# Two of a batch's four loads issued from ScalarE's DMA queue, in a grouped-query attention forward and backward

## The chip, the cores and the metric

The kernel runs on one core of a Trainium2 chip. A core has TensorE (matrix products; PE in the profile, PEld for its weight loads), VectorE (DVE), ScalarE (ACT), GpSimd (POOL) and SyncE (SP), each with its own instruction stream, and sixteen DMA engines that move data between HBM and SBUF. A DMA transfer is issued by an instruction on one of these streams and ends when its semaphore has received sixteen arrivals, one from each DMA engine. The metric is the device time of one execution in microseconds, lower is better; it is given as the median of several runs.

## The reference

Attention of 4 query positions against 2048 keys, 32 batches, 32 query heads on 4 key heads, and its gradients. Everything is bfloat16 at the interface.

```python
B, Hq, Hkv, Sq, Sk, D = 32, 32, 4, 4, 2048, 128
k = jnp.repeat(k, 8, axis=1); v = jnp.repeat(v, 8, axis=1)
scores = jnp.einsum("bhqd,bhkd->bhqk", q, k) * D ** -0.5
p = softmax(scores, axis=-1)
out = jnp.einsum("bhqk,bhkd->bhqd", p, v)
# returned: out, and the gradients of q, k and v for a given grad_out
```

The 8 query heads of a key head times 4 positions make 32 rows; the 4 key heads together fill 128 partitions. Each batch reads K and V (2 MB each) and writes their gradients (2 MB each), so HBM traffic is 273 MB in all, half read and half written.

## The kernel before

**Data.** The host packs K and V of a batch into two rows each: heads 0 and 1, and heads 2 and 3. A row is 128 partitions by 4096 bf16 values. The K rows are 128 values longer: the first K row carries q of the batch, the second grad_out. The gradients leave in the same form, the second dK row with dq and the second dV row with the output appended. So a batch has eight transfers of about 1 MB: four loads and four stores. In SBUF there are 20 row slots; a slot holds a loaded row, and later a row of results or another load.

**Steps of a batch.** The plan names them with two letters or a little more, a part number and a place:

- `LK` 0 and 1, `LV` 1 and 0: the loads, first and second K row, and the V rows, row 1 ahead of row 0. They are called LK0, LK1, LV1 and LV0 in what follows. `SV` 1 and 0, `SK` 0 and 1: the stores of dV and dK, called SV1, SV0, SK0 and SK1.
- `QT`, `KT`, `VT`, `ET`, `DT`: transposes on TensorE into PSUM (line 241, for q and grad_out line 230); `KTe` and so on copy the result to SBUF on ScalarE (line 207) or VectorE (line 209).
- `S`: scores (line 255); `MX`, `EX`, `RC`: maximum, exponential with row sums (ScalarE, line 264), reciprocal.
- `O`, `DQ` (line 288): output and dq. `DP`, `DL`, `DS`: gradient of the scores. `DV`, `DK` (line 310): gradients, copied out of PSUM into a result row by `DVe` and `DKe` (line 316) on ScalarE or VectorE. `dop`, `qp`, `rs` are small products on GpSimd.

**Order.** There is no loop over batches in the usual sense. `PLAN` is a string of four characters per step: name, part, place (PSUM bank, engine A or D, or SBUF slot) and tile. `plan()` turns it into a list of units, and `emit(u)` issues them one after another under a manual schedule, so the string fixes the order on every engine. Steps of three batches interleave: stores and late steps of one batch stand between early steps of the next and loads of one to three batches ahead. In the later part of the plan the eight transfers of a cycle stand in this order: SV1, LV0, SV0, LK1, SK0, LV1, LK0, SK1.

**Queue.** All transfers are issued by SyncE (`nc.sync.dma_start`, line 226 for loads, line 320 for stores), so they form one queue. The waits are put in by the framework: a load waits until the readers of its slot are done, or the store from its slot has landed, and a store waits for the copies into its row. Transfers take eight completion semaphores in turn, and a transfer also waits until the transfer that had its semaphore before, eight places earlier, has landed; with eight transfers per batch that is the same transfer of the batch before. An instruction that waits holds back everything behind it on its engine. SyncE has nothing else to do than these issues; ScalarE's stream consists of the copies of lines 207 and 316 and the exponential.

The first batch's loads are split in two halves each.

Of the kernel before, what the change touches and what calls it, by code (L numbers as in the profile page):

```python
# [160 lines left out]
def kernel(  # L161
# [11 lines left out]
    nc = tc.nc  # L173
# [40 lines left out]
    def emit(u):  # L214
        b, name, i = u.b, u.name, u.part
        t = T[b]
        if name in ("LK", "LV"):
            x = slots[int(u.where, 36)]
# [4 lines left out]
            n = LONG if name == "LK" else ROW  # L223
            src = (k_r if name == "LK" else v_r)[i][b]
            for w in (slice(0, Sk), slice(Sk, n)) if b == 0 else (slice(0, n),):
                nc.sync.dma_start(out=x[:, w], in_=src[:, w])  # L226
        elif name == "QT":
            ps = t["qtp"] = bank(u)[:, 0:P]
            for j, x in enumerate(("q", "go")):
# [4 lines left out]
        elif name in ("KT", "VT", "ET", "DT"):  # L234
# [3 lines left out]
            src = t[x, h] if h is not None else t["e" if x == "E" else "ds"][:]  # L238
            src = src.bitcast(FP32).rearrange("p (j d) -> p j d", d=P)
# [4 lines left out]
        elif name in ("S", "DP"):  # L244
# [6 lines left out]
            out = t["S"][:, 2 * QW * i:2 * QW * i + 2 * QW] if name == "S" else t["DP", i]  # L251
            x, side = ("KT", 0) if name == "S" else ("VT", 1)
# [26 lines left out]
        elif name in ("O", "DQ"):  # L279
            if i == 0:  # L280
                t[name] = bank(u)[:, 0:D]
            xt, x = ("ET", "V") if name == "O" else ("DT", "K")
# [7 lines left out]
        elif name in ("Oe", "DQe"):  # L290
            x, by, to = ("o", "rinv", "DV") if name == "Oe" else ("dq", "rs", "DK")
# [9 lines left out]
        elif name == "DS":  # L301
            w = slice(2 * QW * i, 2 * QW * i + 2 * QW)
            nc.vector.scalar_tensor_tensor(out=t["ds"][:, w], in0=t["DP", i], scalar=t["dl"][:], in1=t["e"][:, w],  # L303
                                           op0=ALU.subtract, op1=ALU.mult)
        elif name in ("DV", "DK"):
            i, g = divmod(i, 2)
# [6 lines left out]
        elif name in ("DVe", "DKe"):  # L313
            i, g = divmod(i, 2)
            copy = nc.scalar.copy if u.where == "A" else nc.vector.tensor_copy
            copy(out=heads_of(t[name[:2], "out", g])[:, :, QW * i:QW * i + QW],  # L316
                 in_=t[name[:2], i, g].rearrange("p (h c) -> p h c", h=2))
# [4 lines left out]
    with tc.manual_schedule():  # L322
        for u in units:
            emit(u)
# [37 lines left out]
```

## Time and profile before

| | us |
|---|---|
| timed runs (median, lowest, highest of 3) | 671.31, 671.30, 671.62 |
| span of the profiled execution | 671.1 |
| PE busy in it | 607.9 |
| VectorE busy | 572.0 |
| ScalarE busy | 569.6 |
| GpSimd busy | 39.0 |

The span runs from the first to the last instruction of one profiled execution; a time for this execution apart from its span is not given. The page cuts the span into 40 slices and shows the busy share of each in tenths, the granted TensorE clock, the share of the DMA engines and what they moved:

```profile
PE   6998999999998999988998989988999989898993
DMA  9999999999999999999999999999999999999867
GB/s 354 417 424 423 419 381 423 423 423 423 423 426 424 424 423 424 424 425 426 414 420 425 413 417 421 414 422 424 396 388 408 417 424 424 404 421 423 347 258 322
```

The single transfers, from issue to landing (lines of KB each and median us):

```profile
out_dram<-row SPq DMA_DIRECT2D x64, 1056.0 KB, 20.1
out_dram<-row SPq DMA_DIRECT2D x64, 1024.0 KB, 20.4
row<-in_k_dram SPq DMA_DIRECT2D x62, 1056.0 KB, 18.1
row<-in_v_dram SPq DMA_DIRECT2D x62, 1024.0 KB, 20.5
```

A transfer of 1 MB takes some 20 us from issue to landing because up to seven others stand ahead of it in the queue.

### The profile page before, as it was taken

The page shows a single profiled execution, that of the slowest core. Times are in us where ns is not written, and L with a number is a line of the kernel's source. Part 1 is how long each engine was busy: PE and PEld are TensorE (multiplying, and loading weights), DVE is VectorE, ACT ScalarE, POOL GpSimd, SP SyncE. Part 2 cuts the span into 40 slices and gives each one's busy share as a digit, 9 for nine tenths or more (in the row PEclk, how much of TensorE's full clock was granted, in tenths as well). Part 3 has the DMA queues.
Part 4 walks back from the last instruction along what each step waited for, and adds up shares of the span by engine and source line. Part 5 has one row for each costly group of instructions (what it writes and reads, how often), then busy time and mean ns, then how long its engine had stood idle before and what let it go on. Part 6 is the DMA issues. An engine that isn't in the chain of part 4 may idle for free.

```text
span 671.1 us, 20678 instructions
## 1 busy us (share of the span) xinstructions
PE 607.9 (91%) x8768; PEld 401.4 (60%) x8768; DVE 572.0 (85%) x736; ACT 569.6 (85%) x802; POOL 39.0 (6%) x102
## 2 busy tenths in 40 slices
PE   6998999999998999988998989988999989898993
PEld 5665566666665666655655655655655666565651
DVE  1988799999997999988888989887888979896994
ACT  4997899999997999888888989887888979886894
POOL 0000000000000000000000000000000000000000
PEclk9999999999998999999999999998999989998997
DMA  9999999999999999999999999999999999999867
GB/s 354 417 424 423 419 381 423 423 423 423 423 426 424 424 423 424 424 425 426 414 420 425 413 417 421 414 422 424 396 388 408 417 424 424 404 421 423 347 258 322
DMA packets 37533, 273.97 MB, mean 408 GB/s; under 512 B 4160, under 2 KB 4160, under 8 KB 5184
## 3 DMA queue, kind: packets, MB, share of 16 engines
q1 hardware_dynamic: 37440, 272.65, 98.2%
q8 instruction: 69, 1.13, 0.6%
q14 instruction: 24, 0.20, 0.1%
HBM read 136.31 MB, written 136.31 MB: 406 GB/s over the span
## 4 chain that ended last, share of the span: by engine, by line
DMA 50%; PE 37%; DVE 4%; ACT 4%; issue 3%; SPq 0%; POOL 0%; DVEq 0%; ACTq 0%; POOLq 0%
DMA row<-in_k_dram 50%; PE psum L241 19%; PE psum L310 8%; PE psum L288 5%; PE psum L255 5%; ACT row L316 3%; DVE vt_sb L209 2%; DVE ds_sb L303 1%; DVE row L316 0%; DVE e_sb L260 0%; ACT e_sb L264 0%; PE psum L230 0%; SPq L226 0%; ACT dt_sb L207 0%; DVE row L296 0%
## 5 line engine op out<-in xcount | busy, mean ns | idle before, releaser
L241 PE MATMUL psum<-ident,row 128*128 128x128 f32 x2048 | 290.1, 284 | 28.4 <-DMA row<-in_k_dram 21.5
L316 ACT CAST row<-psum 128x1024 bf16<-128x1024 f32 x292 | 289.2, 1023 | 30.9 <-PE psum L310 29.1
L241 PEld LDWEIGHTS psum<-ident,row 128*128 128x128 f32 x2048 | 224.7, 143 | 94.8 <-issue 32.0
L316 DVE CAST row<-psum 128x1024 bf16<-128x1024 f32 x220 | 264.9, 1217 | 5.7 <-PE psum L310 2.9
L207 ACT COPY kt_sb<-psum 128x512 f32<-128x512 f32 x190 | 110.2, 598 | 20.6 <-PE psum L241 20.4
L207 ACT COPY vt_sb<-psum 128x512 f32<-128x512 f32 x160 | 92.0, 602 | 35.3 <-PE psum L241 34.6
L303 DVE SCALAR_TENSOR_TENSOR ds_sb<-psum,delta,e_sb 128x1024 bf16<-128x1024 f32 x64 | 82.1, 1283 | 13.4 <-PE psum L255 9.0
L310 PE MATMUL psum<-ds_sb,qp_sb 32*128 32x512 bf16 x512 | 76.9, 383 | 3.4 <-ACT row L316 1.0
L260 DVE TENSOR_SCALAR_CACHE_REDUCE e_sb<-psum 128x2048 bf16<-128x2048 f32 x32 | 73.3, 2292 | 5.7 <-PE psum L255 5.7
L310 PE MATMUL psum<-e_sb,dop_sb 32*128 32x512 bf16 x512 | 68.8, 388 | 2.5 <-issue 1.0
L209 DVE COPY kt_sb<-psum 128x1024 bf16<-128x1024 bf16 x66 | 45.0, 685 | 28.4 <-PE psum L241 27.8
L209 DVE COPY vt_sb<-psum 128x1024 bf16<-128x1024 bf16 x96 | 60.7, 684 | 10.0 <-PE psum L241 9.8
L264 ACT ACTIVATE e_sb<-psum,m 128x2048 bf16<-128x2048 f32 x32 | 64.0, 2001 | 0.2 <-DVE e_sb L260 0.2
L271 POOL TENSOR_SCALAR dop_sb<-row,rinv 128x128 bf16<-128x128 bf16 x32 | 19.3, 603 | 605.3 <-DVE rinv L268 530.3
L241 PE MATMUL psum<-ident,ds_sb 128*128 128x128 f32 x256 | 41.8, 286 | 9.6 <-DVE vt_sb L209 7.0
L288 PE MATMUL psum<-row,dt_sb 128*32 128x128 bf16 x2048 | 43.5, 222 | 6.2 <-issue 5.6
L310 PEld LDWEIGHTS <-qp_sb 32*128 32x128 bf16 x512 | 19.4, 91 | 46.1 <-issue 42.6
L255 PE MATMUL psum<-vt_sb,qdt_sb 128*32 128x512 bf16 x512 | 40.7, 388 | 4.6 <-issue 4.5
L288 PEld LDWEIGHTS <-dt_sb 128*32 128x32 bf16 x2048 | 30.8, 95 | 22.0 <-issue 21.1
L241 PEld LDWEIGHTS psum<-ident,ds_sb 128*128 128x128 f32 x256 | 26.9, 140 | 27.2 <-DVE vt_sb L209 16.4
L207 ACT COPY dt_sb<-psum 128x512 f32<-128x512 f32 x63 | 38.4, 611 | 1.0 <-PE psum L241 0.9
L288 PEld LDWEIGHTS <-et_sb 128*32 128x32 bf16 x2048 | 30.4, 95 | 13.8 <-ACT et_sb L207 11.3
(29 smaller groups left out, 310.1 us busy)
## 6 DMA issues: line engine op xcount, KB each, us to landing
out_dram<-row SPq DMA_DIRECT2D x64, 1056.0 KB, 20.1
out_dram<-row SPq DMA_DIRECT2D x64, 1024.0 KB, 20.4
row<-in_k_dram SPq DMA_DIRECT2D x62, 1056.0 KB, 18.1
row<-in_v_dram SPq DMA_DIRECT2D x62, 1024.0 KB, 20.5
row<-in_v_dram SPq DMA_DIRECT2D x4, 512.0 KB, 9.4
row<-in_k_dram SPq DMA_DIRECT2D x2, 544.0 KB, 5.3
row<-in_k_dram SPq DMA_DIRECT2D x2, 512.0 KB, 4.4
```

What stands on the lines that cost most here:

```text
L207: nc.scalar.copy(out=out.bitcast(FP32), in_=in_)
L209: nc.vector.tensor_copy(out=out, in_=in_.bitcast(BF16))
L241: nc.tensor.transpose(out=ps[:, P * j:P * j + P], in_=src[:, 4 * half + j, :], identity=ident32[:])
L255: nc.tensor.matmul(out[r, QW * w:QW * w + QW], lhsT=t["qdt"][:, P * side + 32 * h:P * side + 32 * h + 32], rhs=t[x, NH * i + h][:, QW * w: ...
L260: nc.vector.tensor_scalar(out=t["e"][:], in0=t["S"], scalar1=-scale, scalar2=None, op0=ALU.mult, op1=ALU.min, accum_out=t["m"][:])
L264: nc.scalar.activation(out=t["e"][:], in_=t["S"], func=ACT.Exp, bias=t["m"][:], scale=scale, accum_out=t["l"][:])
L271: nc.gpsimd.tensor_scalar(out=t["dop"][:], in0=t["go"], scalar1=t["rinv"][:], scalar2=None, op0=ALU.mult)
L288: nc.tensor.matmul(t[name][r, :], lhsT=left[:, j, r, odd], rhs=right[:, 4 * i + j, :, odd], start=(i == 0 and c == 0), stop=(i == 1 and c ...
L303: nc.vector.scalar_tensor_tensor(out=t["ds"][:, w], in0=t["DP", i], scalar=t["dl"][:], in1=t["e"][:, w], op0=ALU.subtract, op1=ALU.mult)
L310: nc.tensor.matmul(acc[:, QW * (h % 2):QW * (h % 2) + QW], lhsT=t[still][rows[h], :], rhs=t[moving][rows[h], QW * i:QW * i + QW], start=Tr ...
L316: copy(out=heads_of(t[name[:2], "out", g])[:, :, QW * i:QW * i + QW], in_=t[name[:2], i, g].rearrange("p (h c) -> p h c", h=2))
```

## The change

From batch 4 on, two of the four loads of a batch, LK1 and LV0, are issued by ScalarE with `nc.scalar.dma_start`, which puts them on ScalarE's hardware DMA queue. The plan string, the slots and every computation stay. The other six transfers of a batch, and all loads of batches 0 to 3, remain with SyncE. 56 transfers move. They now stand in ScalarE's stream at the place that the plan gives them, between its copies: LK1 ahead of a copy of a V tile, LV0 ahead of a copy of a K tile.

```diff
             src = (k_r if name == "LK" else v_r)[i][b]
             for w in (slice(0, Sk), slice(Sk, n)) if b == 0 else (slice(0, n),):
-                nc.sync.dma_start(out=x[:, w], in_=src[:, w])
+                queue = nc.scalar if b >= 4 and (name, i) in (("LK", 1), ("LV", 0)) else nc.sync
+                queue.dma_start(out=x[:, w], in_=src[:, w])
```

In the compiled program of the changed kernel each of the 56 issues on ScalarE waits for the same load of the batch before (its semaphore), and in part for an older load into its slot or for GpSimd's reading of it. SyncE keeps 204 of its 260 issues; per batch their order is SV1, SV0, SK0, LV1, LK0, SK1. Otherwise the order of instructions on the engines is that of before.

## The prediction

> **What bounds the kernel now.** I read the page's DMA part first, then busy time by stage, then SP's own waits, TensorE's waits, the chain of waits, and last the issue times of single transfers.
>
> ```profile
> DMA packets 37533, 273.97 MB, mean 408 GB/s; under 512 B 4160, under 2 KB 4160, under 8 KB 5184
> q1 hardware_dynamic: 37440, 272.65, 98.2%
> q8 instruction: 69, 1.13, 0.6%
> ```
>
> One queue carries everything and its packets fill 98.2% of the sixteen engines' span. The stages (columns after the window: its length, then PE, PEld, DVE, ACT and POOL busy, clock, DMA share, GB/s):
>
> ```profile
> 100.00:255.00 155.00, 149.17 (x2188) 98.04 (x2185) 142.36 (x184) 140.02 (x199) 9.58 (x24) 0.99 1.01 424
> 255.00:606.00 351.00, 320.67 (x4669) 211.98 (x4666) 307.11 (x395) 302.36 (x430) 20.38 (x52) 0.99 1.01 417
> 606.00:671.00 65.00, 50.51 (x802) 31.72 (x802) 47.52 (x60) 48.15 (x65) 3.56 (x9) 0.92 0.81 336
> ```
>
> From 100 to 255 us compute is nearly full (PE 149 of 155) and lives on data loaded ahead: the exponential that starts a batch recurs every 18.9 us (234.44, then 253.32). From 255 to 606 us the DMA sets the pace; a batch takes 20.5 us, 17.1 batches in the stage. SP's and then TensorE's waits between 260 and 600 us (total, times, longest):
>
> ```profile
> SPq L320 <- DMA out_dram<-row: 98.3, 49, 2.2
> SPq L226 <- DMA out_dram<-row: 83.7, 17, 5.6
> SPq L226 <- DMA row<-in_v_dram: 67.4, 33, 2.1
> SPq L226 <- DMA row<-in_k_dram: 35.4, 16, 2.8
> SPq L320 <- ACT row L316: 2.7, 6, 1.0
> ```
> ```profile
> PE psum L241 <- DMA row<-in_k_dram: 14.2, 12, 2.1
> ```
>
> SP waits 285 of 340 us for transfers eight places earlier, hardly ever for data: the window of eight is always full. TensorE waits about 1.2 us a batch for one K load. The chain says which:
>
> ```profile
> 565.38 20.47 DMA row<-in_k_dram
> ...
> 585.92 20.43 DMA row<-in_k_dram
> 606.35 0.14 issue
> 606.49 1.94 PE psum L241 x16
> ```
>
> Second K load of batch 29, then of batch 30, each issued when its predecessor lands; TensorE takes up the last 0.14 us after its landing. Matched by the plan, from 255 to 606 us the second K load (LK1) lands mostly 0.2 us before its first use and the last V load (LV0) mostly 0.1 to 1.5 us, while the other V load (LV1) has 4.5 to 7 us and the first K load (LK0) 6 to 10. The change moves the two with no slack.
>
> What sets the 20.5 us is **one DMA engine**. The trace holds sixteen arrivals per transfer, one an engine. In this stage the first comes some 7.5 us after issue, the fifteenth by 13, the last at 20.5. Intervals between successive last arrivals are, by role, 2.45 to 2.54 us (medians) for loads and 2.59 to 2.70 for stores; the engine that is first needed 2.42 to 2.56 for loads and 2.44 to 2.54 for stores between 110 and 255 us, while it was never held up. So the last engine is slow on stores only, by 0.14 us each (means of the differences), and it works without a gap from 110 us until the last store lands (640.1, 642.7, 645.9, 648.5 ... 667.5, 670.0). A rearrangement can't shorten the kernel unless this engine does its 260 transfers in less time.
>
> **The change part by part.** *SP loses 56 issues* of 0.34 us (rows below), 19 us; SP's time is waiting, so 0. Its order becomes SV1, SV0, SK0, LV1, LK0, SK1, and each waits for the same transfer of the batch before; LK0 still waits for the SK1 in its slot, and SK0 now names the moved load that filled its slot batches ago, which has long landed. Six are in flight where eight were, 15 us of work for the last engine (6 x 2.57): it does not run dry, 0.
>
> *ScalarE gains 56 issues.* No ScalarE issue is in the trace. Bounds: 0, if its sequencer issues while a copy still runs, and 1.67 us, SP's longest. I take SP's median:
>
> ```profile
> 544.82 0.34 SPq L226 DMA_DIRECT2D row<-in_k_dram  x1
> ...
> 549.78 0.34 SPq L226 DMA_DIRECT2D row<-in_v_dram  x1
> ...
> 560.28 0.34 SPq L226 DMA_DIRECT2D row<-in_v_dram  x1
> ```
> ```profile
> 536.42 1.11 ACT L207 COPY vt_sb<-psum 128x512 f32<-128x512 f32 x2
> ```
>
> 0.68 us a batch. In the DMA stage ScalarE idles 351 - 302.4 = 48.6 us, 2.8 a batch, and the pace leaves 20.5 - 18.9 = 1.6: hidden. Without that cover it would be 17.1 x 0.68 = 11.6 us. From 100 to 255 us a batch grows to 19.6 us, still under 20.5, and eats lead that the DMA stage takes anyway: 0. After 606 us one issue (LV0 of batch 31) is left: **+0.3**.
>
> *The moved loads go out earlier.* ScalarE came to the place of LK1 of batch 28 at 536.42 (the copy above is the one behind it), SP issued it at 544.82; to that of LV0 at 554.60, SP at 560.28. Slots are no hindrance: from batch 8 on they last held loads, read long before; for batches 4 to 7 the store in LV0's slot landed 6 to 11 us before ScalarE came by. On a queue of their own, served in turn with SP's, the loads share with at most one transfer each and land some 2 x 2.57 + 2 = 7 us after issue, not 20. TensorE's 1.2 us waits end.
>
> *Who is late next.* The engines do the same work, so two transfers brought forward push the rest back by 2 x 2.57 = 5.1 us. LV1, with 4.5 to 7 us, takes LK1's place. For batch 29, the last inside the stage, it has 5.3 us (landing 590.9, first use 596.2): slack 0.2. Bounds: -1.6 (a batch's spare time comes back at the end) to +0.5; I take **0**, as the stores that end the kernel go through the last engine, which has no gap to give.
>
> *The last engine.* While a moved load is served in turn with a store, store packets alternate with load packets. If its slow stores come from the writing side, that time is covered. 56 loads, each beside one SP transfer, four of six of these stores: 37 x 0.14 = 5.2 us. Bounds: -9.6 us (all of its lag in the stage, 17.1 x 4 x 0.14) and +18, if each change of queue costs 0.04 us (the longest instruction fetch against their mean, below), eight packets for each of 56 loads. The mean itself leaves nothing for a change, so the value lies on the gain's side, between 0 and 5.2; I take half: **-2.6**.
>
> Sum: 671.1 + 0.3 - 2.6 = 668.8 us of span. The profiled execution's time is known by its span alone; the median of the timed runs is 671.31, 0.2 above, so **669.0 us**.
>
> How the engines serve two queues decides all this. The trace has two already: the 69 instruction fetches of q8, 64 us in all (0.6% of 16 x 671), 0.93 each (0.88 to 0.97) for 16 KB, where 8 KB takes 0.31 on q1: 0.62 of its own and one q1 packet between, though q1 had 13 to 20 us of backlog. So two queues are taken in turn, at least for a single packet; for two long queues no row shows it. With a third queue a fetch takes 0.31 us more; the chain stops on a fetch three times (62.83, 201.42, 612.43 us, some 2 us each), and only the last, when no moved load is in flight, lies after the DMA stage: 0. The Trainium skill, "DMA: Bandwidth & Descriptors", section "Queues, rings and completion order", says so too: an engine goes round the queues that have work, a packet at a time; by that rule the second rival below falls away and the forecast's sum stays, and the fetches agree with 0.93 us.
>
> **Rivals.** *1. Hidden anyway (no change).* The last engine's work is the same whichever queue feeds it, LV1 replaces LK1, and the end is where it was: 671.3. For it: no gap in that engine's arrivals; against it: only that its stores, not its loads, are slow. The Trainium skill's page just named, section "Issuing engines are not separate DMA queues", has it thus: both queues run on the same sixteen engines and only issue time is saved; by it the time would be 671.3, and nothing here contradicts it.
>
> *2. ScalarE stands at a load (slower).* Both moved loads wait for the same load of the batch before. If the engines keep to SP's queue first, so that it lands no sooner than now, ScalarE stands as SP does: 544.82 - 536.42 = 8.4 us at LK1, with the copies of V tiles behind it whose PSUM banks TensorE needs. The delay is taken once, not per batch, as the pace stays 20.5: 671.3 + 8.4 = 679.7; where the tail absorbs half, 675.5. It decides once a moved load takes over 20.5 us, the time between two issues of its kind, to land; for it, that SP's transfers take 20.4 now; against it, the fetch row.
>
> *3. ScalarE's issue is dear (slower).* Above 1.6 / 2 = 0.8 us each, compute becomes the bound of the stage: at 1.0 us 17.1 x 0.4 = 7 us, 678; SP's first issues behind one another show 0.8 to 1.7 us a few times, 0.34 nearly always.
>
> *4. The last engine loses its lag wholly:* 671.3 - 9.6 = 661.7.
>
> **Chances.** Forecast 0.37, rival 1 0.29, rival 2 0.16, rival 3 with dearer queue changes 0.13, rival 4 0.05. About 0.2% (1.3 us) is what can be told from no change. The forecast's own range is 666 to 670.5, a little of it (0.02) within 0.2%; rivals 2 and 3 are slower but for 0.02. So faster 0.40, same 0.33, slower 0.27. The range 663.5 to 678 leaves out rival 4 and the upper part of rivals 2 and 3.
>
> **What would show it.** Right: two hardware queues, the new one with 56 transfers' bytes (some 58 MB); moved loads land in about 7 us; TensorE's wait for K is gone and one for V (LV1) appears; ScalarE's DMA issues about 0.34 us with no wait before them; last arrivals of stores nearer 2.5 us. Wrong: ScalarE idle for several us ahead of its issues (rival 2), issues near 1 us (3), a batch still 20.5 us with stores at 2.6 to 2.7 (1). The prediction fails above all if DMA packets grow longer than 309 and 319 ns when two queues are interleaved.

## The result and the profile after

The change made the kernel slower: 675.52 us (median of 4, 674.87 to 676.84) against 671.46 before (median of 4, 671.30 to 672.24), ratio 1.0053, 95% interval 1.0035 to 1.0071. The profiled execution took 674.87 us, its span is 673.1. Where a run's time and span are both known, the time is mostly 1.7 to 2.5 us above the span, so the profiled execution of the kernel before, of which only the span (671.1) is known, took some 673 us, above the four runs given here (671.30 to 672.24). The two profiles are thus 2.0 us of span apart, while the medians are 4.1 apart: half of the loss can be seen in them.

The DMA part of the page of the changed kernel (queue: packets, MB, share of 16 engines):

```profile
DMA packets 37532, 273.96 MB, mean 407 GB/s; under 512 B 4160, under 2 KB 4160, under 8 KB 5184
q1 hardware_dynamic: 29376, 213.01, 76.5%
q10 hardware_dynamic: 8064, 59.64, 21.6%
q8 instruction: 68, 1.11, 0.6%
```

The same bytes now travel on two queues, and 76.5 + 21.6 = 98.1% of the engines' span is filled, as before (98.2). From the issue list, with the median from issue to landing last, and from ScalarE's order of work:

```profile
row<-in_k_dram ACTq DMA_DIRECT2D x28, 1056.0 KB, 11.1
row<-in_v_dram ACTq DMA_DIRECT2D x28, 1024.0 KB, 9.7
```
```profile
557.65 1.01 ACT L317 CAST row<-psum 128x1024 bf16<-128x1024 f32 x1
557.73 0.34 ACTq L227 DMA_DIRECT2D row<-in_v_dram  x1
558.56 1.08 ACT L207 COPY kt_sb<-psum 128x512 f32<-128x512 f32 x2
```

The moved loads land in 10 to 11 us where they took 18 to 20; ScalarE's issue takes 0.34 us, lies inside the copy that still runs, and nothing waits ahead of it. The stages, in the columns of before (length, busy times, clock, DMA share, GB/s):

```profile
100.00:255.00 155.00, 147.18 (x2186) 97.37 (x2184) 141.69 (x183) 138.85 (x199) 9.57 (x24) 1.00 1.01 424
255.00:606.00 351.00, 317.14 (x4634) 210.57 (x4632) 302.54 (x388) 294.39 (x421) 20.34 (x51) 0.97 1.01 415
606.00:673.10 67.10, 54.11 (x846) 34.38 (x842) 53.04 (x68) 53.40 (x73) 3.59 (x9) 0.96 0.81 332
```

The DMA stage moves 415 GB/s in place of 417, and at its end more compute is left: VectorE has 53.04 us of work after 606 us where it had 47.52, ScalarE 53.40 where it had 48.15. The granted clock, 0.97 in the stage where it was 0.99, doesn't explain the loss: after 606 us it is higher than before (0.96 against 0.92), and the kernel with LK1 alone moved (e1 below) had 1.00 in the stage and lost as much. Cut at 500 us, before first, then after:

```profile
255.00:500.00 245.00, 223.02 (x3276) 147.08 (x3274) 213.65 (x273) 209.90 (x299) 14.36 (x36) 0.99 1.01 417
500.00:606.00 106.00, 97.66 (x1395) 64.91 (x1393) 93.46 (x123) 92.46 (x132) 6.01 (x16) 0.98 1.01 416
```
```profile
255.00:500.00 245.00, 220.92 (x3258) 147.03 (x3260) 211.65 (x273) 206.17 (x296) 14.36 (x36) 0.97 1.01 417
500.00:606.00 106.00, 96.22 (x1384) 63.54 (x1376) 90.89 (x116) 88.22 (x126) 5.99 (x15) 0.95 1.01 411
```

Up to 500 us the DMA is as fast as before. What it loses, it loses in the last 106 us of the stage: 5 of 416 GB/s, 1.3 us. SP's waits between 260 and 600 us, and two waits between 255 and 606 us that the list of the kernel before does not show (total, times, longest):

```profile
SPq L321 <- DMA out_dram<-row: 168.5, 46, 5.2
SPq L227 <- DMA out_dram<-row: 78.9, 16, 5.6
SPq L227 <- DMA row<-in_v_dram: 34.5, 17, 2.0
SPq L321 <- DVE vt_sb L209: 14.0, 3, 4.7
```
```profile
ACT row L317 <- DMA out_dram<-row: 31.4, 17, 3.0
PE psum L311 <- ACT row L317: 27.4, 17, 2.8
```

SP still waits for transfers, not for its own time. TensorE's wait for the K load (14.2 us before) is no longer among its waits in this stage; in its place ScalarE waits once a batch, 1.8 us each, for a store to land before it may write the next result into that slot, and TensorE waits for ScalarE. By the plan this is the slot of the store SK0, which the first result copy of SV1 two batches later takes over. In the kernel before, this copy already had no time to spare: from 255 to 606 us it starts 0.08 us behind that store's landing in 13 of 17 batches. TensorE's product for it was ready less than 0.1 us earlier, so that the list puts the short wait down to TensorE:

```profile
ACT row L316 <- PE psum L310: 17.2, 34, 1.1
```

In the changed kernel it is 0.08 us in all 17, and TensorE's product was ready up to 1.7 us earlier. The store lands some 4 us later (batch 16: 386.1 us against 381.6; batch 25: 572.5 against 567.9). The exponential of batch 28 starts at 585.9 us against 581.5, that of batch 31 at 649.6 against 646.1, and the last store lands at 671.9 against 670.0.

### The profile page after: what moved, and what is told of

Its sections match the earlier page's. It is cut to its first block, busy times and chain, and to the rows that moved or that the text cites. A ratio compares the mean times of both kernels' runs of the same rounds, so it can differ in the third digit from the quotient of the medians.

```text
span 673.1 us, 20644 instructions
## 1 busy us (share of the span) xinstructions
PE 605.6 (90%) x8768; PEld 402.2 (60%) x8768; DVE 572.1 (85%) x736; ACT 565.7 (84%) x802; POOL 39.0 (6%) x102
## 3 DMA queue, kind: packets, MB, share of 16 engines
q1 hardware_dynamic: 29376, 213.01, 76.5%
q10 hardware_dynamic: 8064, 59.64, 21.6%
## 4 chain that ended last, share of the span: by engine, by line
DMA 71%; PE 20%; ACT 4%; DVE 3%; issue 1%; POOL 0%; SPq 0%; DVEq 0%; ACTq 0%; POOLq 0%
DMA row<-in_v_dram 69%; PE psum L242 10%; PE psum L311 5%; PE psum L289 3%; DMA row<-in_k_dram 3%; ACT row L317 3%; PE psum L256 2%; DVE vt_sb L209 1%; DVE ds_sb L304 1%; DVE row L317 0%; ACT kt_sb L207 0%; ACT e_sb L265 0%; ACT vt_sb L207 0%; ACT dt_sb L207 0%; DVE row L297 0%
## 5 line engine op out<-in xcount | busy, mean ns | idle before, releaser
L311 PE MATMUL psum<-e_sb,dop_sb 32*128 32x512 bf16 x512 | 63.6, 392 | 30.1 <-ACT row L317 29.7
L209 DVE COPY kt_sb<-psum 128x1024 bf16<-128x1024 bf16 x66 | 44.9, 683 | 12.1 <-PE psum L242 11.8
L311 PEld LDWEIGHTS <-dop_sb 32*128 32x128 bf16 x512 | 16.6, 91 | 53.9 <-issue 44.4
L289 PE MATMUL psum<-row,dt_sb 128*32 128x128 bf16 x2048 | 45.7, 232 | 3.2 <-issue 2.6
L256 PE MATMUL psum<-vt_sb,qdt_sb 128*32 128x512 bf16 x512 | 42.7, 406 | 3.9 <-issue 3.8
L289 PEld LDWEIGHTS <-dt_sb 128*32 128x32 bf16 x2048 | 32.9, 100 | 19.3 <-issue 18.4
## 6 DMA issues: line engine op xcount, KB each, us to landing
row<-in_k_dram ACTq DMA_DIRECT2D x28, 1056.0 KB, 11.1
```

Of the source, the lines that this page charges most:

```text
L209: nc.vector.tensor_copy(out=out, in_=in_.bitcast(BF16))
L256: nc.tensor.matmul(out[r, QW * w:QW * w + QW], lhsT=t["qdt"][:, P * side + 32 * h:P * side + 32 * h + 32], rhs=t[x, NH * i + h][:, QW * w: ...
L289: nc.tensor.matmul(t[name][r, :], lhsT=left[:, j, r, odd], rhs=right[:, 4 * i + j, :, odd], start=(i == 0 and c == 0), stop=(i == 1 and c ...
L311: nc.tensor.matmul(acc[:, QW * (h % 2):QW * (h % 2) + QW], lhsT=t[still][rows[h], :], rhs=t[moving][rows[h], QW * i:QW * i + QW], start=Tr ...
```

## The experiments

Eighteen kernels were run, each beside runs of the kernel before on the same chip (medians 671.99 us for e1 to e4, 672.21 for e5 to e8, 671.64 for e9 to e12, 672.30 for e13 to e16, 672.21 for e17 and e18). Ratios are to these, with 95% intervals. "Lengthening" below is worked out from the trace's packet records: what a packet of 8448 or 8192 B takes above 319 or 309 ns, summed and divided by sixteen engines.

The expectations name their theories. *Slot* and *critical-transfer* theory: what costs is a transfer without slack that the moved loads pass, the store SK0 first of all. *Two-queue* theory: a second queue in itself slows the engines. *Mix* and *bunching* theory: packets grow when most engines load at once, so what counts is how loads and stores mix. *End* theory: only what is left of the lag when the loads run out costs time.

**e1: only the second K load on ScalarE's queue.**

```diff
-                queue = nc.scalar if b >= 4 and (name, i) in (("LK", 1), ("LV", 0)) else nc.sync
+                queue = nc.scalar if b >= 4 and (name, i) in (("LK", 1),) else nc.sync
```

> From batch 4 on only the second K load (LK1) goes out on ScalarE's queue. Slot theory: a load brought forward pushes every transfer it passes back by one service of the slowest engine, 2.57 us; the store SK0, whose slot ScalarE's next result copy writes with 0.1 us to spare, is passed by one load instead of two, so ScalarE waits for a store's landing and the time is about half way, 672.7 to 674.5. Rival, the DMA engines lose time whenever two queues are served: also about half, 673.5. Rival, ScalarE's issue is dear: half too. By itself it tells only whether LK1 or LV0 carries the loss.

676.34 us, 1.0066 (1.0052 to 1.0080).

**e2: only the last V load.**

```diff
-                queue = nc.scalar if b >= 4 and (name, i) in (("LK", 1), ("LV", 0)) else nc.sync
+                queue = nc.scalar if b >= 4 and (name, i) in (("LV", 0),) else nc.sync
```

> From batch 4 on only the last V load (LV0) goes out on ScalarE's queue. Slot theory: SK0 is passed by one load, 672.7 to 674.5, with ScalarE waiting for a store's landing. Rivals: half the loss too. If one of the two kernels has the whole loss and the other none, the loss isn't the number of transfers that pass the store but something of that load.

672.68 us, 1.0014 (1.0002 to 1.0026). The halves are not equal: one load alone costs all that both cost, the other a third of it or less. e1 waits in stage 255 to 606 us:

```profile
ACT row L317 <- DMA out_dram<-row: 25.2, 17, 2.2
...
PEld psum L242 <- DMA row<-in_v_dram: 14.1, 14, 2.3
```

Beside the store, the load that was left on SP's queue is now late. In e2, where no wait of ScalarE for a store is listed, TensorE still waits for the K load, 17.2 us in 13 times. The number of loads that pass SK0 is not the measure of its delay: in batch 25 it lands 5.0 us later than before in e1, with one load moved, 0.6 in e2, also with one, and 4.5 in the change, with two.

**e3, e4: another slot for the late store's successor**, with the change (e3) and without it (e4). Two slots change places, so that from batch 9 on the result row of SV1 takes over the slot of the SV1 two batches before, whose store lands some 10 us earlier than SK0 (batch 16 in the change: 376.5 us against 386.1):

```diff
+        x, y = slot(used), slot(freed)
+        for key, k in at.items():
+            if starts[key] >= p:
+                units[k].where = {x: y, y: x}.get(units[k].where, units[k].where)
...
-    units = plan()
+    units = reslot(plan())
```

> The changed kernel, with two slots exchanged from about batch 6 on: the result row of SV1 takes the slot that SV1 of two batches before left (free some 10 us earlier), and the load LV1 takes the one that SK0 left. Same transfers, same queues, same instruction order. Slot theory: ScalarE's wait for stores (33 us, 20 times) nearly goes, the next limits are the slot of SV0 (1.6 to 4.2 us) and LV1 (4.5 us), and the time falls by 2 to 4 us against the changed kernel, to 671.5 to 673.5. Rivals (two queues make the engines slower; ScalarE's issue is dear): it stays at 675.5, as queues and issues are the same.

> The kernel before, with the same two slots exchanged and all transfers on SyncE's queue. Slot theory: SK0 landed 0.1 us before ScalarE's copy there too, but LK1 (0.2 us) and LV0 (0.1 us) bind at the same pace, so it stays at 671.4 within 0.8. If SK0 alone had bound, it would fall by 1 to 2 us. Rivals: 671.4.

e3 679.78 us, 1.0119 (1.0105 to 1.0133); e4 672.09, 1.0005 (0.9996 to 1.0014). A miss for the theory of the one slot: ScalarE's wait for the store is nearly gone in e3 (3.7 us in all), but VectorE now waits for one, and the time rose:

```profile
PE psum L336 <- DVE row L342: 19.7, 12, 2.4
DVE row L342 <- DMA out_dram<-row: 18.4, 10, 2.3
```

Removing the one wait does not bring the time back; it looks like the place where the compute meets a DMA that is behind, and not like the cause of the loss. The packet records of these runs led to the next theory: the engines are busy throughout the stage in all of them, and what differs is the lengthening (e2 6.7 us, before 8.0, the change 8.6, e3 10.5, e1 11.9).

**e5, e6: the order alone, on SP's queue.** e5 moves LK0 behind the store SK1 that follows it, e6 moves SV0 behind the LK1 that follows it, from batch 4 on:

```diff
+        first, then = [next(k for k, u in enumerate(units) if (u.name, u.part, u.b) == key) for key in (("LK", 0, b), ("SK", 1, b - 3))]
+        if first < then:
+            units.insert(then, units.pop(first))
...
-    units = plan()
+    units = moved(plan())
```

with `(("SV", 0, b - 3), ("LK", 1, b))` in e6.

> Before, all on SP's queue, with the first K load moved behind the store SK1 that follows it, so that SP's list alternates a store and a load throughout (S L S L S L S L in place of L S S L S L S L). Mix theory (what the runs so far suggest: the 16 DMA engines are never idle from 255 to 606 us, and what differs is how much longer than 309 or 319 ns their packets take, 8.0 us per engine in this stretch before, 11.9 with LK1 alone moved; packets lengthen when most engines load at the same time, so what counts is how loads and stores are mixed, not which queue carries them): the lengthening falls from 8.0 to 4-8 us, time 668 to 671.5. Two-queue theory (a second queue itself slows the engines): no change, 671.5 to 672.5. Critical-transfer theory (what counts is which transfer with no slack is passed): SK1 lands one transfer earlier, LK0 has 6 us to spare, so 671 to 672.5.

> Before, all on SP's queue, with the store SV0 moved behind the load LK1 that follows it, so that SP's list goes in pairs (L L S S L L S S). Mix theory: more engines load at once, the lengthening of packets from 255 to 606 us rises from 8.0 to 9-12 us per engine, time 673 to 676 with one queue alone. Two-queue theory: no change, 671.5 to 672.5. Critical-transfer theory: LK1, which has 0.2 us of slack, comes one transfer (2.57 us) earlier and SV0 has 5.2 us to its next use: 669 to 672.

e5 742.64 us, 1.1044 (1.1006 to 1.1082); e6 689.18, 1.0261 (1.0239 to 1.0283). e5 is a miss for every theory, e6 in the direction of the mix theory and four times its size. Three moments of e5, with DMA share and GB/s last, and a wait of SP and of TensorE from 255 to 606 us:

```profile
308.00:310.00 2.00, 2.00 (x21) 1.62 (x19) 2.00 (x4) 1.99 (x4) 0.86 (x3) 1.00 0.39 164
312.00:314.00 2.00, 2.00 (x70) 1.15 (x70) 1.97 (x5) 1.96 (x3) 0.00 (x0) 1.00 0.98 258
315.00:317.00 2.00, 2.00 (x21) 1.50 (x19) 2.00 (x2) 1.65 (x3) 0.00 (x0) 1.00 1.02 417
```
```profile
SPq L328 <- DVE row L324: 176.0, 16, 13.3
```
```profile
PE psum L249 <- DMA row<-in_k_dram: 40.1, 14, 4.2
```

SP now stands once a batch at the store SK0 until its data are there, up to 13.3 us, and some 4 us more at SK1, which now holds LK0 back; the queue runs dry (308 to 310 us: share 0.39). All engines then start the next transfer together, and from 312 to 314 us they are full (0.98) and yet move 258 GB/s. All row packets of these 2 us have 8192 B (a K load has 8448), and by the arrivals nearly all engines write the store SK0; a packet takes 496 ns on average in place of 309. From 315 us, mostly on the V load behind it, they move 417. That an alternating list mixes loads and stores was wrong: it does only while the engines are at different places of the list. And packets grow in e5 where nearly all engines write as well as where they load, which the mix theory did not have.

**e7: all four stores of batches 4 to 28 on ScalarE's queue,** each behind ScalarE's next instruction.

```diff
-            nc.sync.dma_start(out=(dv_r
+            queue = nc.scalar if 4 <= b < 29 else nc.sync
+            queue.dma_start(out=(dv_r
```

> Before, with all four stores of the batches 4 to 28 issued by ScalarE, each behind ScalarE's next instruction, and all loads left to SP. Mix theory: each engine then takes a packet of a load and one of a store in turn while both queues hold work, so near half of the engines load at any time; the lengthening falls to 2-6 us per engine, time 666 to 671, unless ScalarE is held at a store by its data, which would show as ScalarE's waits. Two-queue theory: twice as many transfers as in the change are on the second queue, so slower than the change: 676 to 682.

690.25 us, 1.0269 (1.0250 to 1.0288): as the two-queue theory had it but for its size, and lengthening 12.1 us. SP, left with the loads, waits up to 14.4 us for the stores whose slots they need (before: 5.6), so more than the queue has changed here.

**e8: only LV1, the load with 4.5 us and more to spare, on ScalarE's queue.**

```diff
-                queue = nc.scalar if b >= 4 and (name, i) in (("LK", 1), ("LV", 0)) else nc.sync
+                queue = nc.scalar if b >= 4 and (name, i) in (("LV", 1),) else nc.sync
```

> The change with another load: LV1 alone, which has 4.5 us or more of slack, is issued by ScalarE from batch 4 on; 28 transfers on the second queue, as where LK1 alone was moved (676.3) or LV0 alone (672.7). Mix theory: SP's list without it alternates but for one pair of stores, so the lengthening stays at 7-9 us and the time at 670.5 to 673. Two-queue theory: as LK1 alone, 675 to 677. Critical-transfer theory: SK0, with 0.1 us of slack, is passed by one transfer (2.57 us), 673.5 to 675.

675.96 us, 1.0055 (1.0037 to 1.0074), lengthening 10.0. Having slack does not make a load free to move.

**e9 to e12: K rows 8704 B apart in DRAM in place of 8448**, in the change, before, e5 and e1.

```diff
-    k = [_np.concatenate([k[g], small[g]], axis=-1) for g in range(2)]
+    k = [_np.concatenate([k[g], small[g], _np.zeros_like(small[g])], axis=-1) for g in range(2)]
```

> The change, with each K row of the input (8448 B, the K rows with q or the output gradient behind them) lying 8704 B apart in DRAM in place of 8448 B; the same bytes are loaded. Theory of K loads in step (from the packets of the runs so far, 255 to 606 us: where ten or more of the 16 DMA engines read K rows at once, a packet took 12 to 90 ns longer than its 319 ns, where fewer than four do 3 to 14; such moments hold 22% of the packets of the change, 24% with LK1 alone, 0.1% of the kernel before), in the form that the distance of the rows in DRAM makes them clash: the lengthening falls from 8.5 us to 3-5 us, time 669 to 673. If the distance is not the cause: 675 to 676.5, as the change. Two-queue theory: as the change.

> Before, with the same distance of 8704 B between the K rows. Theory of K loads in step with the distance as cause: the kernel before has hardly any moment with ten engines on K rows, but 59% of its packets with four to ten at 10 to 12 ns more each; the lengthening falls from 8.0 to 3-5 us and the time to 667 to 670. If the distance is not the cause: 671.5 to 672.5.

> The kernel whose SP list alternates (742.6), with the same distance between the K rows; it has the most lengthening (28 us in 255 to 606, 90 ns per packet where 13 or more engines read K rows). Theory of K loads in step with the distance as cause: the lengthening falls below 10 us and the time to 700 to 722 (the queue running dry once a batch, 15 us of idle in this stretch, stays). If the distance is not the cause: 738 to 747.

> LK1 alone on ScalarE's queue (676.3), with the same distance between the K rows. Theory of K loads in step with the distance as cause: the lengthening falls from 11.9 to 4-6 us, time 669 to 673. If the distance is not the cause: 675.5 to 677. Two-queue theory: 675.5 to 677.

676.56 us (1.0070, 1.0044 to 1.0096), 672.36 (1.0003, 0.9994 to 1.0013), 745.10 (1.1080, 1.1043 to 1.1118) and 674.64 (1.0038, 1.0023 to 1.0053). This distance of the rows is not the cause; e12 lies 1.7 us under e1, too little for that theory (669 to 673) and outside the other range (675.5 to 677) too. e9 and e10 serve as second profiles of the two kernels.

**e13, e14: the change in some batches only**, 4 to 23 in e13; in e14, with `if b >= 24 and`, the last eight.

```diff
-                queue = nc.scalar if b >= 4 and (name, i) in (("LK", 1), ("LV", 0)) else nc.sync
+                queue = nc.scalar if 4 <= b < 24 and (name, i) in (("LK", 1), ("LV", 0)) else nc.sync
```

> The change for the batches 4 to 23 only; from 24 on all loads are SP's again. Bunching theory (the traces show that the two loads on the second queue are served together with LV1 and LK0 of SP's queue, four loads at a time and then four stores at a time; loads served by most engines at once take longer packets, and engines now and then have nothing: about 1.4 us per engine over the 17 batches from 255 to 606 us): the loss comes batch by batch, so some 11 of 17 parts of it here, 673 to 675. End theory (a store that the compute waits for lands some 4 us later, and only what is left of that when the loads run out costs time): the last batches go in the old order, so no loss, 671 to 672.5. Two-queue theory: 20 of 28 parts, 674 to 675.5.

> The change from batch 24 on only. Bunching theory: some 6 of 17 parts of the loss in the stretch, 672.5 to 674. End theory: the whole loss, 674.5 to 676.5. Two-queue theory: 8 of 28 parts, 672.5 to 673.5.

e13 673.68 us, 1.0018 (1.0004 to 1.0032), as the bunching theory had it; e14 675.61, 1.0046 (1.0030 to 1.0063), as the end theory had it. Twenty batches cost some 1.4 us, the last eight, moved alone, 3.3. From 500 to 606 us, e13 and then e14:

```profile
500.00:606.00 106.00, 100.95 (x1429) 67.08 (x1427) 96.02 (x123) 94.55 (x135) 6.01 (x15) 0.98 1.01 419
```
```profile
500.00:606.00 106.00, 96.61 (x1398) 64.39 (x1397) 91.63 (x118) 90.04 (x129) 6.01 (x15) 0.97 0.99 404
```

With the last loads back on SP the DMA recovers to 419 GB/s; with only the last loads moved it falls to 404. But e14 has a loss of its own, which the change does not have. The completion semaphores are handed out in turn, and here they no longer fall on the same transfer of the batch before: LK1 of batch 27 has the one that the store SV0 of batch 23 used, and ScalarE stands 6.2 us at it. The results come late, SP stands 12.2 us at a store, and the engines are half empty from 534 to 538 us (a wait of ScalarE, one of SP, and this stretch with DMA share and GB/s last):

```profile
ACT vt_sb L207 <- DMA out_dram<-row: 6.2, 1, 6.2
```
```profile
SPq L321 <- DVE row L317: 12.2, 1, 12.2
```
```profile
534.00:538.00 4.00, 4.00 (x90) 3.01 (x92) 3.97 (x6) 3.92 (x7) 1.20 (x3) 1.00 0.52 214
```

So the 3.3 us of e14 are not the price of the last eight batches in the change. What these cost there, e13 tells: without the move in them the ratio falls from 1.0053 to 1.0018.

**e15, e16: the change with both loads issued 12 or 6 of ScalarE's instructions later.**

```diff
+            u, left = units.pop(k), 12
+            while left:
+                left -= on_act(units[k])
+                k += 1
+            units.insert(k, u)
```

> The change, with both loads issued by ScalarE 12 of its instructions (some 10 us) later than in the change, so that by the traces they should be served while SP's queue has its four stores in a row; both have 16 us or more to spare in the change. Bunching theory: loads and stores mix again, the lengthening from 255 to 606 us is at or below the 8.0 us of before and the time 668 to 672. Two-queue theory: 675 to 677, as the change. End theory: the store that the compute waits for is passed by fewer loads, 671 to 673.

> The same with 6 instructions (some 5 us). Bunching theory: half mixed, 671 to 675. Two-queue theory: 675 to 677. End theory: 672 to 674.5.

e15 675.34 us, 1.0049 (1.0022 to 1.0075), lengthening 9.4; e16 675.02, 1.0033 (1.0016 to 1.0051), 10.0. Both as the two-queue theory had it, a miss for the end theory and for the bunching theory (e16 at the edge of its range): the later issue did not bring the packets back to their length.

**e17, e18: the reverse at the end**, on SP's queue: LK0 behind the LV0 that follows it, for batches 28 to 31 and 30 to 31 (the edit of e5 with `(("LK", 0, b), ("LV", 0, b - 1))`).

> Before, all on SP's queue, with the load LK0 of the batches 28 to 31 moved behind the load LV0 that follows it three places on (it lands 7 to 11 us before its first use, three places are 7.7 us). The end theory turned round: SK1, SV1 and LV0, the last with next to no slack, go one place (2.57 us) earlier at the end, the compute is less behind when the loads run out: 669 to 671.5. If LK0 now comes too late, TensorE waits for it by its row and the time is 673 to 677. Bunching theory: one place in four batches is nothing, 671.5 to 673.

> The same for the batches 30 and 31 alone. End theory: 669.5 to 672, as what counts is the order when the loads run out; if LK0 is late, 672.5 to 675. Bunching theory: 671.5 to 673.

673.11 us, 1.0015 (1.0005 to 1.0025), and 672.70, 1.0009 (1.0000 to 1.0018). No gain, so a miss for the end theory, and no late LK0 either (TensorE waits 4.4 and 3.0 us for K loads from 540 to 640 us, 4.1 before). None of the eighteen beat the kernel before.

**All together.** From the profiles: MB that SP's and ScalarE's queues moved from 255 to 606 us, lengthening from 255 to 500 and from 500 to 606 us, GB/s from 500 to 606 us, VectorE's work left after 606 us, and, worked out from the sixteen arrivals of each transfer, how many transfers the first engine is ahead of the eighth from 550 to 606 us (times are medians, from different chips):

```
kernel            time    MB      length.    GB/s  left  ahead
before           671.46  145.56  5.3  2.7    416   47.5  1.6
e4 other slots   672.09  145.85  5.0  2.5    417   46.8  1.7
e10 padded       672.36  145.79  5.2  2.3    417   47.0  1.4
e18 LK0 from 30  672.70  146.52  3.9  2.1    418   47.6  1.5
e17 LK0 from 28  673.11  146.50  4.4  1.6    421   47.6  2.1
e2 LV0 only      672.68  146.03  4.4  2.3    417   48.7  1.0
e13 b 4-23       673.68  146.01  4.5  2.0    419   48.6  0.6
e12 LK1 padded   674.64  144.27  7.1  3.3    411   51.2  0.4
e16 held 6       675.02  144.59  6.7  3.3    412   51.9  0.8
e15 held 12      675.34  144.92  5.4  4.1    410   50.8  1.0
the change       675.52  145.09  4.9  3.6    411   53.0  0.3
e14 b 24-31      675.61  143.80  5.7  3.5    404   52.6  0.3
e8 LV1 only      675.96  144.64  5.2  4.8    406   53.8  1.0
e1 LK1 only      676.34  143.81  8.3  3.6    412   51.9  1.0
e9 change padded 676.56  145.17  5.3  3.1    413   52.9  0.6
e3 change, slots 679.78  144.33  6.5  3.9    409   53.4  0.3
```

e5, e6, e7 and e11, all at 689 us or above, are left out. The others fall into two groups with nothing between: up to 673.7 us with 416 to 421 GB/s from 500 to 606 us and at most 48.7 us of VectorE's work left, and from 674.6 us with 404 to 413 and at least 50.8. Every kernel of the second group has a second queue in use up to the last batches; of the first only e2 has.

## Why the prediction was wrong

*What bounds the kernel:* right. The sixteen engines are full from 100 to 606 us in the change as before (DMA share 1.01), and SP's waits are for transfers. Two readings were loose: 83.7 of SP's 285 us are LK0's wait for the store SK1 in its slot, seven places earlier and not eight, and TensorE's 1.2 us for a K load came in 12 of the 17 batches.

*SP's 56 issues, ScalarE's 56 issues:* right. 0.33 to 0.38 us each, inside a running copy, no wait ahead; ScalarE is busy 8 us less in the DMA stage, because its work lags, and 5 us more after it. The second rival (ScalarE stands at a load) and the third (a dear issue) are out, though the time lies where the second had put it (675.5), by chance: ScalarE does stand, 1.8 us a batch, but at a result copy.

*Six in flight do not run dry:* nearly. In the stage the engines had some 0.5 us each without work, more than in the kernel before (packet times summed over the profiles of the change and e9 against those of before, e4 and e10).

*The moved loads land in 7 us:* mis-sized, 10 to 11. LK1 goes out 3.8 us after LV0 (median) and finds it ahead on its own queue: LV0 of batch 28 was issued at 557.73 and landed at 566.63, LK1 of batch 29 at 561.70 and 572.31. The 2 us in the prediction's sum stood without a row. The Trainium skill, "DMA: Bandwidth & Descriptors", section "Queues, rings and completion order", has an engine take the queues in turn; the two landing times, 11.1 and 9.7 us beside 20 for what SP issues, agree with it.

***Who is late next* failed.** The prediction named LV1, with a slack of 0.2 us, and took 0. It looked at loads alone. The transfer with no slack that the two loads passed was the store SK0, whose landing ScalarE's copy into its slot followed by 0.08 us in the kernel before already: it came some 4 us later (the prediction reckoned 5.1 for the transfers passed), and the compute with it. LV1 never came closer than 4.5 us. But e3 took this wait away and got slower, so it is not the whole price.

***The last engine* failed** (-2.6). Nothing was covered; the interval of its arrivals went from 20.67 to 20.75 us a batch, and it still took 2.70 us for the store SK1. What the text named as its main risk came: packets longer than 309 and 319 ns. From 500 to 606 us they are 3.1 to 3.6 us longer in the change and e9, 2.3 to 2.7 in before, e4 and e10.

The loss that the profiles show, by their means: spans 672.8 (change, e9) against 670.6 (before, e4, e10), 2.2 us. From 255 to 606 us the engines have moved 145.13 MB in place of 145.73; 0.60 MB at 0.415 MB per us is 1.4 us, of it some 0.8 longer packets and 0.5 empty engines; 0.48 of the 0.60 MB are lost after 500 us. The other 0.8 comes after 606 us, where 5 to 6 us more of VectorE's work is left and no loads lie beside it. That most of it goes with the last eight batches, e13 shows.

The rival *hidden anyway* (671.3, no change) is out too. The Trainium skill's section "Issuing engines are not separate DMA queues", on the page just named, says that a second issuer saves issue time alone. That the sixteen engines are shared, all runs agree with; but the second queue also changes in which order they serve the transfers, and the change cost 0.5%. That order can cost this and more, e5 and e6 show on a single queue. That it is the order which cost it here is not shown: the theory that a second queue costs in itself fits e8, e15 and e16, and what speaks against it is that e1 and e2, with 28 transfers each on the second queue, have ratios of 1.0066 and 1.0014.

How the bunching looks, in the changed kernel, 8 us in which nearly only stores are served, then 8 us of loads (DMA share and GB/s last), and below it the same stretches before, which are mixed:

```profile
404.00:412.00 8.00, 5.88 (x155) 3.62 (x153) 4.52 (x9) 4.47 (x6) 0.22 (x1) 0.79 1.00 417
414.00:422.00 8.00, 7.88 (x76) 5.15 (x74) 7.46 (x9) 7.45 (x13) 0.00 (x0) 1.00 0.99 380
```
```profile
404.00:412.00 8.00, 7.96 (x128) 5.08 (x121) 7.39 (x11) 7.40 (x12) 0.00 (x0) 1.00 1.02 425
414.00:422.00 8.00, 6.17 (x50) 4.62 (x48) 6.36 (x9) 6.73 (x11) 1.20 (x3) 1.00 1.01 419
```

In these four the compute differs as well; it is the DMA that the figures are shown for. With the two loads gone from SP's list, four stores stand in a row there, SK1, SV1, SV0 and SK0, and the loads of the second queue are served along with LV1 and LK0. In the stage 33% of the packets start while under a tenth of the engines load (1.9 ns longer each) and 29% while over nine tenths do (15.7 ns); in the kernel before it is 1% and 2%. Yet the bunching alone is not the loss. By the same reckoning, with its limits (it goes by the arrivals), over nine tenths load for 1% of the packets of e8 and 4% of those of e15, and both are as slow as the change.

*What stays open.* The cause of the loss as a whole: no theory of the expectations fits all runs. Why packets grow when most engines load at once, in the change those of K loads on SP's queue more than those of V loads, and in e5 those of stores too (the distance of the rows is not it; what else in the memory it might be was not tried). Why the loss sets in near 500 us: the engines of the change fall into step, from 1.3 transfers between the first and the eighth (255 to 350 us) to 0.3, and so do those of e3, e12 and e14, but e1, e8, e15 and e16 are slow without it. And half of the difference of the medians, as the profiled executions of the change were among its fastest.

## What to carry to other kernels

Where the DMA engines have no gap, a second queue adds nothing to serve with; it reorders, and every transfer brought forward pushes another back, so look for the next one without slack among the stores whose slots the compute will write, too. Even with the same bytes on one queue the order has a price of its own, as e5 and e6 show: don't let a store that waits for data hold loads behind it in the same list. And look at the rate near the end, where the lag of the compute is no longer covered by loads. When an edit changes which transfers are on which queue, look at which transfer each one now waits for before you read its time (e14).

## What the runs showed of the hardware

- One place in one list can cost ten per cent: e5 differs from the kernel before by LK0 and SK1 changing places, and takes 742.6 us where the kernel before takes 672.2.
- Engines that are all busy can move 258 GB/s or 417 (e5, two stretches of 2 us): the one on a store, all engines in step, the other mostly on a V load.
- Where under a tenth of the engines load, packets keep their time to within 2 ns in the change; where over nine tenths load, a packet took 16 ns more there, 32 in e1 and some 60 to 80 in e5. In e5, with the engines in step, packets took as much longer, some 75 to 90 ns, where under a tenth load.
- A DMA issue of ScalarE runs while its copy before still runs: issued at 557.73, inside the copy from 557.65 to 558.66.
